# Phase 1 reads x by features for its last five pairs of token tiles: no transposes on TensorE, one multiplication on VectorE

## The chip, the cores and the metric

The kernel runs on one core of one Trainium2 chip. The metric is the device time of one execution, in microseconds (us). Lower is better.

## The reference

One transformer block over S = 2048 tokens of width D = 640, in float32. The change touches only the first line of the work: the layer norm of x, and the three projections that read it.

```python
mod = (silu(c) @ w_mod).reshape(6 parts of 640)      # sa, ca, ga, sb, cb, gb
h = layernorm(x) * (1 + ca) + sa                     # phase 1 starts here
q, k, v = h @ wqkv                                   # 32 heads of 20
phi_q, phi_k = [softmax(z), softmax(-z)] of q @ w_phi, k @ w_phi, per head
o = phi_q (phi_k^T v) / (phi_q sum(phi_k) + 1e-6)    # linear attention
x = x + ga * (o @ wo)
h = layernorm(x) * (1 + cb) + sb
x = x + gb * (relu(h @ w1 + b1)^2 @ w2 + b2)
```

layernorm subtracts the mean over the 640 features and divides by sqrt(variance + 1e-5).

## The kernel before

The 2048 tokens are 16 tiles of 128 (t = 0 to 15) and 8 pairs of tiles. Names in the code count pairs from 0: `hT7`, `xb7` belong to the pair that the title of the change calls pair 8, so its pairs 4 to 8 are j = 3 to 7. This text counts from 0 throughout.

Phase 1 makes, for every tile, k, v and (up to tile 11) q. TensorE multiplies with the tokens as the stationary operand, so it needs the normed x with features on partitions. That is `hT[j]`: five chunks of 128 features, each in a high part (rounded) and a low part (the rest), for the 256 tokens of a pair. Each product is three matmuls (high with high, high with low, low with high), and the third one of a chunk reads the low part. `proj` does one tile: 15 matmuls of 384 columns, then 15 of 256.

How `hT` comes about before the change. `load_x` brings 256 tokens (tokens on partitions). `ln_parts` gets mean and variance by accumulating activations on ScalarE (L339, L344), the small arithmetic on GpSimd, and then normalises in place on ScalarE (L350). `t1(j, chunks)` transposes a chunk on TensorE (L363, two 128x128 per chunk, into the PSUM tile `ta`), and `t_out` takes it out: ScalarE scales and shifts it (L374, to `hfa`), ScalarE rounds it to the high part (L375, to `hT`), and VectorE subtracts to get the low part (`lo`, L89 `hT<-hfa,hT`).

Around it, per tile: ScalarE copies k and q out of PSUM (L431) and v into `vt` (L424 to L427). VectorE takes each head's maximum and minimum (L435, L436: `mxk`, `mxq`), subtracts them (L438: `ek`, `eq`, two each), ScalarE takes exponentials (L441, L442), and VectorE sums k's (`sk`, L446), inverts (L447) and multiplies (L448), and sums q's (`rs_q`, L483). `do_kv` multiplies `ek` with `vt` into `kvp`, two tiles at a time, at every even tile from 2 on between its v and its q. On the side run the modulation vectors (`wm`, L295 and L297 on VectorE; `mc` and a last column on TensorE) and, from tile 9 on, the weights of the output projection (`rwo`, `wo`). Tiles 12 to 15 get their q after phase 1.

The order of the work in this stretch: TensorE's is as written in the code (`manual_schedule`). On VectorE, ScalarE, GpSimd and SyncE a scheduler sorts the instructions when the kernel is built, within the constraints of `tc.issue_after`. What comes out is one fixed queue per engine: an instruction that waits holds up all that stand behind it. The tags of the tiles set the number of buffers: `ek` has two, `hT` two, XB two.

Of the kernel before, what the change touches and what calls it, by code (L numbers as in the profile page):

```python
# [8 lines left out]
F32 = mybir.dt.float32  # L9
# [24 lines left out]
POSTPONED = 4  # L34
WARM = 9
KEPT = NT - POSTPONED
W2_AT = 48
PLAIN = 2
DEALT = range(NT // 2)
# [13 lines left out]
def kernel(  # L53
    ctx: ExitStack,
    tc: tile.TileContext,
    x: bass.AP,
    wk5: bass.AP,
    wk1: bass.AP,
    wq5: bass.AP,
# [79 lines left out]
    def tp(name):  # L139
        return psA.tile([P, 512], F32, tag="tp", name=name)  # L140
# [78 lines left out]
                nc.sync.dma_start(raw[nm][2][:40, 1], w1)  # L219

    def load_x(j):
        XB[j] = tok2(f"x{j % 2}", f"xb{j}")
        nc.sync.dma_start(XB[j], x[256 * j : 256 * j + 256].rearrange("(i p) d -> p i d", p=P))

    def load_wm(d):
        WM[d] = flat(tok2(("k", "k", "q0", "q1", "w")[d], f"wm_{d}"))
# [74 lines left out]
    def mod_turn(part, p, *cs_):  # L301
        t = MT.setdefault(part, None) or row("s1", f"mt{part}")
        MT[part] = t
        a, n = cs_[0] * P, len(cs_) * P
        for i, c in enumerate(cs_):
            src = by_turn(MA[part])[:, c] if part in (3, 4) else MA[part][:, c * P : (c + 1) * P]
            nc.tensor.transpose(p[:, i * P : (i + 1) * P], src, ident)
        nc.scalar.activation(t[:, a : a + n], p[:, :n], AF.Copy)
# [24 lines left out]
    def ln_parts(xt, nm, spare=None):  # L333
# [16 lines left out]
            nc.scalar.activation(xt[:, i], xt[:, i], AF.Identity, bias=nb[:, i : i + 1], scale=sq[:, i : i + 1])  # L350
        yield

    def layer_norm(xt, nm, spare=None):
        for _ in ln_parts(xt, nm, spare):
            pass
# [29 lines left out]

    DONE = []

    def t1(j, *ds, more=None):
        if 0 in ds:
            HT[j] = ht(f"hT{j}", j)  # L390
        p = tp(f"ta{j}_{ds[0]}")
        for k, d in enumerate(ds):
            t_in(XB[j], d, p[:, 256 * k : 256 * k + 256])
        if more:
            mod_turn(more[0], p[:, 256:], 4)
# [3 lines left out]
        if more:  # L399
            mod_sum(*more)  # L400

    def proj(nm, t, between=None):
        p = pj(f"p{nm}{t}")
# [123 lines left out]
    def wo_weights(*gs):  # L527
# [189 lines left out]
    pe.__enter__()  # L717
    for t in range(2, NT - 2):
        j, i = divmod(t, 2)
        if i == 0 and j < NT // 2 - 2:  # L720
            load_x(j + 2)
        PK[t] = row("s2", f"k{t}")
        to_sb(proj("k", t), PK[t])
        if t == NT - 4:
            t1(j + 1, 0, 1)
        norm = j + 1 if i == 0 and t < NT - 4 else j + 2 if t == NT - 5 else None
        if norm:
            if not i:
                parts = ln_parts(XB[norm], f"a{norm}")
            with tc.issue_after(newest(ET_.Activation)):  # L730
                next(parts)
        p = proj("v", t, (1, 0, lambda: t1(j + 1, 4)) if t == NT - 3 else None)
# [6 lines left out]
        if norm and not i:  # L739
# [4 lines left out]
        if norm and not i:  # L744
            next(parts)
        if i and t < NT - 4:
            t1(j + 1, 2, 3)
        with tc.issue_after(newest(ET_.DVE)):
            k_norm(EK[t], t)
        if t < NT - POSTPONED:  # L750
            do_q(t, (1, 3, lambda: t1(j + 1, 4, more=LAST_COL.get(t))) if i else None)
            if norm and i:
                with tc.issue_after(newest(ET_.Activation)), tc.issue_after(DONE[0]):
                    next(parts)
            if i:
                with tc.issue_after(DONE[1]):
                    q_chain(t)
            else:
                q_chain(t)
        if i == 0 and t < NT - 4:  # L760
            t1(j + 1, 0, 1)
        if t == NT - 6:
            parts = ln_parts(XB[j + 2], f"a{j + 2}")
            with tc.issue_after(newest(ET_.Activation)):
                next(parts)
        SIDE[t]()
    pe.__exit__(None, None, None)
    behind.close()
# [944 lines left out]
    by_hand.__exit__(None, None, None)  # L1713


_INS = ["x", "wk5", "wk1", "wq5", "wq1", "wv", "bd", "c", "w_ss", "w_mod", "wo", "w1", "b1", "w2", "b2"]


# [53 lines left out]
```

## Time and profile before

| | us |
|---|---|
| three runs | 755.70, 755.99, 756.49 |
| median of the runs | 755.99 |
| span of the profiled execution | 754.9 |
| TensorE busy in the span | 749.6 (99%) |
| VectorE busy | 607.5 (80%) |
| ScalarE busy | 458.8 (61%) |
| GpSimd busy | 170.4 (23%) |

The profile gives no time of its own for the profiled execution beside its span; the median of the runs is 1.1 us above the span, and that is taken as what lies around it. The granted TensorE clock is 1.000 throughout. Phase 1 with the five pairs in question lies at about 92 to 233 us of the span. "Busy" counts overlapped instructions once; a matmul's end is modelled, so that a TensorE that is always busy may still issue more slowly than it could. In the rows below, the columns are start, duration, engine, line, operation, output and inputs, count, and in brackets the idle time of the engine before it and who ended it.

### The profile page before, as it was taken

The page shows a single profiled execution, that of the slowest core. Times are in us where ns is not written, and L with a number is a line of the kernel's source. Part 1 is how long each engine was busy: PE and PEld are TensorE (multiplying, and loading weights), DVE is VectorE, ACT ScalarE, POOL GpSimd, SP SyncE. Part 2 cuts the span into 40 slices and gives each one's busy share as a digit, 9 for nine tenths or more (in the row PEclk, how much of TensorE's full clock was granted, in tenths as well). Part 3 has the DMA queues.
Part 4 walks back from the last instruction along what each step waited for, and adds up shares of the span by engine and source line. Part 5 has one row for each costly group of instructions (what it writes and reads, how often), then busy time and mean ns, then how long its engine had stood idle before and what let it go on. Part 6 is the DMA issues. An engine that isn't in the chain of part 4 may idle for free.

```text
span 754.9 us, 15404 instructions
## 1 busy us (share of the span) xinstructions
PE 749.6 (99%) x5888; PEld 731.9 (97%) x5888; DVE 607.5 (80%) x1123; ACT 458.8 (61%) x1060; POOL 170.4 (23%) x365
## 2 busy tenths in 40 slices
PE   9999999999999999999999999999999999999998
PEld 9999999999999998998899999999999999999997
DVE  6598987988999899999755768787777776777766
ACT  5767666677863355556677757485574756647431
POOL 3001101011200237646303030132221313213110
PEclk9999999999999999999999999999999999999999
DMA  9811431342432264664777475897677767667461
GB/s 324 336 39 80 155 96 70 106 139 103 138 105 93 71 190 142 143 153 124 173 204 218 121 216 215 278 326 204 185 213 204 205 196 212 191 181 208 132 188 36
DMA packets 58931, 126.70 MB, mean 168 GB/s; under 512 B 7452, under 2 KB 16417, under 8 KB 58857
## 3 DMA queue, kind: packets, MB, share of 16 engines
q1 hardware_dynamic: 38706, 79.41, 32.1%
q0 software_dynamic: 17568, 41.00, 22.0%
q10 hardware_dynamic: 2583, 5.30, 1.9%
q8 instruction: 46, 0.75, 0.5%
q14 instruction: 28, 0.23, 0.1%
HBM read 100.94 MB, written 29.89 MB: 173 GB/s over the span
## 4 chain that ended last, share of the span: by engine, by line
PE 86%; DVE 11%; POOL 1%; issue 1%; ACT 0%; DVEq 0%; POOLq 0%
PE up L79 24%; PE acc L79 18%; PE pk L79 9%; PE pv L79 9%; PE pq L79 8%; PE acc3x L79 5%; PE pwo L79 3%; PE kvp L455 3%; DVE dn L883 3%; DVE scr L881 2%; DVE ezb L905 2%; PE foldk L281 1%; PE ta L363 1%; DVE ot L89 1%; POOL dn L889 1%; PE foldq L281 1%
## 5 line engine op out<-in xcount | busy, mean ns | idle before, releaser
L79 PE MATMUL up<-h,w 128*128 128x256 f32 x1640 | 204.4, 276 | 0.1
L79 PEld LDWEIGHTS up<-h,w 128*128 128x128 f32 x1640 | 196.4, 188 | 0.5 <-DVE h L89 0.3
L1321 ACT ACTIVATE ft<-up,b_t 128x256 f32<-128x256 f32 x104 | 48.9, 471 | 96.0 <-PE up L79 95.6
L79 PE MATMUL acc<-w,ra 128*128 128x384 f32 x452 | 97.5, 335 | 0.0
L79 PE MATMUL pwo<-wo,ot 128*128 128x256 f32 (+3 forms) x512 | 79.9, 311 | 0.4 <-DVE ot L89 0.4
L1322 DVE TENSOR_TENSOR ft<-ft 128x256 f32<-128x256 f32 x104 | 43.8, 421 | 43.0 <-ACT ft L1321 41.4
L79 PEld LDWEIGHTS pwo<-wo,ot 128*128 128x128 f32 (+1 forms) x512 | 74.3, 188 | 3.5 <-issue 2.7
L79 PE MATMUL pq<-wq,hT 128*128 128x384 f32 (+1 forms) x480 | 75.1, 311 | 0.0
L79 PEld LDWEIGHTS acc<-w,ra 128*128 128x128 f32 x452 | 72.7, 188 | 0.9 <-DVE ra L89 0.6
L79 PE MATMUL pk<-wk,hT 128*128 128x384 f32 (+1 forms) x480 | 72.7, 308 | 0.0
L79 PE MATMUL pv<-wv,hT 128*128 128x384 f32 (+1 forms) x480 | 71.6, 306 | 0.0
L79 PEld LDWEIGHTS pq<-wq,hT 128*128 128x128 f32 x480 | 71.0, 188 | 0.6 <-issue 0.2
L79 PEld LDWEIGHTS pk<-wk,hT 128*128 128x128 f32 x480 | 70.5, 188 | 0.4 <-issue 0.2
L79 PEld LDWEIGHTS pv<-wv,hT 128*128 128x128 f32 x480 | 70.0, 188 | 0.0
L89 DVE TENSOR_TENSOR ra<-ft,ra 128x384 fp32r<-128x384 f32 (+2 forms) x86 | 36.8, 449 | 32.7 <-ACT ra L1345 19.4
L1431 POOL DMA_DIRECT2D ring_a<-td_a x34 | 18.5, 544 | 117.1 <-PE acc L79 103.7
L1345 ACT ACTIVATE ra<-ft 128x384 fp32r<-128x384 f32 x48 | 25.2, 526 | 28.5 <-DVE ft L1322 22.4
L79 PE MATMUL acc3x<-w,ra 128*128 128x256 f32 x231 | 39.5, 278 | 0.0
L79 PEld LDWEIGHTS acc3x<-w,ra 128*128 128x128 f32 x231 | 37.2, 188 | 0.0
L1336 DVE TENSOR_TENSOR ft<-ft 128x128 f32<-128x128 f32 x136 | 33.4, 286 | 1.2
L446 DVE TENSOR_REDUCE sk<-ek 128x64 f32<-128x1280 f32 x16 | 23.7, 1483 | 12.4 <-ACT ek L441 10.8
L889 POOL TENSOR_TENSOR dn<-dn,rs_q 128x32 f32<-128x32 f32 x32 | 19.9, 622 | 59.0 <-DVE dn L883 58.7
(264 smaller groups left out, 1458.2 us busy)
## 6 DMA issues: line engine op xcount, KB each, us to landing
ring_c<-td_c POOLq DMA_DIRECT2D x34, 384.0 KB, 4.1
ring_a<-td_a POOLq DMA_DIRECT2D x34, 384.0 KB, 3.5
ring_b<-td_b POOLq DMA_DIRECT2D x34, 256.0 KB, 3.5
esp<-eq SPq DMA_DIRECT2D x12, 640.0 KB, 3.2
el<-esp SPq DMA_DIRECT2D x12, 640.0 KB, 4.4
rw<-in_w SPq DMA_DIRECT2D x23, 320.0 KB, 3.5
wm<-in_w_mod SPq DMA_DIRECT2D x20, 320.0 KB, 3.7
xb<-in_x SPq DMA_DIRECT2D x8, 640.0 KB, 4.0
```

The costliest lines, as they stand in the source:

```text
L79: nc.tensor.matmul(o, a, b, start=first and i == 0, stop=last and i == len(terms) - 1, skip_group_check=skip,)
L89: (eng or nc.vector).tensor_tensor(out_lo, full, hi.bitcast(F32), op=ALU.subtract)
L281: nc.tensor.matmul(p[g // 3][:, (g % 3) * 120 : (g % 3) * 120 + n], r, bd_t[:120, g * 120 : g * 120 + n], start=True, stop=True,)
L446: nc.vector.tensor_reduce(s, heads(flat(e)), axis=AX.X, op=ALU.add)
L455: nc.tensor.matmul(kvp[g // 4][64 * c : 64 * c + 64, a : a + 2 * n].rearrange("p (s n) -> p s n", s=2), v[:, u], e[:, :, o : o + n], start ...
L883: nc.vector.tensor_reduce(dn.rearrange("p s h -> p (s h)"), heads(z), axis=AX.X, op=ALU.add)
L889: nc.gpsimd.tensor_tensor(dn[:, s], dn[:, s], rs[:, 1 - s], op=ALU.mult)
L1321: nc.scalar.activation(r, p, AF.Relu, bias=b1_t[:, f : f + 1])
L1322: nc.vector.tensor_tensor(r, r, r, op=ALU.mult)
L1336: nc.vector.tensor_tensor(t[:, o], t[:, a], t[:, b], op=op)
L1345: nc.scalar.activation(a[:, 0, :3], t[:, :3], AF.Copy)
L1431: nc.gpsimd.dma_start(RING[j, n, r], TD[n][r].bitcast(F32R))
```

## The change

For pairs 3 to 7, x is also given to the kernel as `x_t`, transposed on the host's side of the input list (features on partitions, 256 tokens in a row). What is done with it:

- `row_parts(j)`: tokens are still loaded (`load_x`, always into the buffer x1) and still go through the two accumulating passes on ScalarE, but only for the statistics. The pass that normalised them is gone. Two small DMAs (`put_rows`) write minus the mean and one over the deviation, a row of 256 numbers each, to DRAM.
- `put_mean(j)`: a DMA from DRAM to DRAM spreads minus the mean over a 128 x 1280 buffer `xd`. `centre(j)`: a DMA issued on GpSimd adds `x_t` to it.
- `load_xt(j)`: a pair later, the centred x comes in as `xt`, and the row of one over the deviation, on all partitions, as `rb`.
- `t1(j, chunks)`: one VectorE multiplication of all five chunks (128 x 1280) by `rb`, in place; then `t_out` reads `xt` where it read PSUM. Chunks 0 to 2 are emitted at the end of the even tile, 3 and 4 in the odd tile, ahead of its spread.
- The last column of the modulation vectors, which shared a transposing group with chunk 4, is a group of its own (`last_col`). The special handling of the last pair (its statistics and chunks earlier than the others', for tiles 11 to 13) is gone: it now runs in the same places as the others.

```diff
+TURNED = 3
+    def put_rows(j, *cols):
+        LR[j] = dram.tile([2, 256], F32, name=f"lr{j}")
+        for k, col in enumerate(cols):
+            nc.sync.dma_start(LR[j][k].rearrange("(i p) -> p i", p=P), col)
+    def put_mean(j):
+        XD[j] = dram.tile([P, NC * 256], F32, name=f"xd{j}")
+        nc.sync.dma_start(
+            XD[j].rearrange("p (d n) -> p d n", d=NC), LR[j][0][None, None, :].to_broadcast([P, NC, 256])
+        )
+    def centre(j):
+        nc.gpsimd.dma_start(XD[j], x_t[j * P : (j + 1) * P], accum_op=ALU.add, max_dma_last_dim=2048)
+    def load_xt(j):
+        XT[j] = flat(tok2("x0", f"xt{j}")).rearrange("p (d n) -> p d n", d=NC)
+        nc.sync.dma_start(XT[j], XD[j].rearrange("p (d n) -> p d n", d=NC))
+        RB[j] = row("s3", f"rb{j}")[:, :256]
+        nc.sync.dma_start(RB[j], LR[j][1][None, :].to_broadcast([P, 256]))
...
+    def row_parts(j):
...
+        for i in range(2):
+            nc.scalar.activation(xt[:, i], xt[:, i], AF.Identity, accum_out=sm[:, i : i + 1])
...
+        for i in range(2):
+            nc.scalar.activation(xt[:, i], xt[:, i], AF.Square, bias=sm[:, i : i + 1], accum_out=sq[:, i : i + 1])
...
+        put_rows(j, sm, sq)
...
-    def t1(j, *ds, more=None):
+    def t1(j, *ds):
...
+        if j >= TURNED:
+            if 0 in ds:
+                with tc.issue_after(newest(ET_.DVE)):
+                    nc.vector.tensor_tensor(XT[j], XT[j], RB[j][:, None, :].to_broadcast([P, NC, 256]), op=ALU.mult)
+            with tc.issue_after(newest(ET_.Activation)):
+                for d in ds:
+                    t_out(cols_a, HT[j], d, f"a{j}", XT[j][:, d], XT[j][:, d])
+            return
         p = tp(f"ta{j}_{ds[0]}")
         for k, d in enumerate(ds):
             t_in(XB[j], d, p[:, 256 * k : 256 * k + 256])
...
-        12: lambda: t1(NT // 2 - 1, 2, 3),
...
     for t in range(2, NT - 2):
         j, i = divmod(t, 2)
-        if i == 0 and j < NT // 2 - 2:
-            load_x(j + 2)
+        norm_by_tokens = j + 1 < TURNED
+        norm = i == 0 and norm_by_tokens
+        new_x = TURNED if norm else j + 3 if i and TURNED < j + 3 < NT // 2 else None
+        centred = TURNED if j + 2 == TURNED and i else j + 2 if TURNED < j + 2 < NT // 2 and not i else None
+        if new_x:
+            load_x(new_x)
+        if centred:
+            put_mean(centred)
+        if i == 0 and j + 1 >= TURNED:
+            load_xt(j + 1)
...
-        if t == NT - 4:
-            t1(j + 1, 0, 1)
-        norm = j + 1 if i == 0 and t < NT - 4 else j + 2 if t == NT - 5 else None
...
+        if i and not norm_by_tokens:
+            t1(j + 1, 3, 4)
         spread(PK[t], EK[t], f"k{t}")
         exps(EK[t])
...
+        if centred:
+            centre(centred)
...
+        if new_x:
+            with tc.issue_after(newest(ET_.Activation)):
+                row_parts(new_x)
+        if i == 0:
+            t1(j + 1, 0, 1, *(() if norm_by_tokens else (2,)))
```

Three places show how the queues change. In the rows, the number behind a name is the tile's or the pair's, and what follows the underscore tells buffers apart; `xt6` and `hT6` are the x and the features of pair 6, which TensorE reads from tile 12 on.

The first place is VectorE's queue in tile 11, where pair 6 is made ready. Before:

```order
L89 TENSOR_TENSOR hT6_2381<-hfa6_0_2387,hT6_2381 128x256
L89 TENSOR_TENSOR hT6_2381<-hfa6_1_2391,hT6_2381 128x256
L504 TENSOR_TENSOR rwo2_2401<-rwo2_2401,ga_b_220 128x640
L438 TENSOR_TENSOR eq10_2371<-q10_2368,mxq10_2372 128x640
L435 TENSOR_REDUCE mxk11_2488<-k11_2409 128x32
L436 TENSOR_REDUCE mxk11_2488<-k11_2409 128x32
L438 TENSOR_TENSOR ek11_2487<-k11_2409,mxk11_2488 128x640
L89 TENSOR_TENSOR wo2_2405<-rwo2_2401,wo2_2405 128x640
L438 TENSOR_TENSOR ek11_2487<-k11_2409,mxk11_2488 128x640
L483 TENSOR_REDUCE rs_q_106<-eq10_2371 128x64
L89 TENSOR_TENSOR hT6_2381<-hfa6_2_2500,hT6_2381 128x256
L89 TENSOR_TENSOR hT6_2381<-hfa6_3_2504,hT6_2381 128x256
```

and now:

```order
L435 TENSOR_TENSOR xt6_2201<-xt6_2201,rb6_2203 128x1280
L484 TENSOR_TENSOR ek11_2453<-k11_2382,mxk11_2460 128x640 x2
L91 TENSOR_TENSOR hT6_2363<-xt6_2201,hT6_2363 128x256 x2
L481 TENSOR_REDUCE mxq11_2511<-q11_2507 128x32
L482 TENSOR_REDUCE mxq11_2511<-q11_2507 128x32
L492 TENSOR_REDUCE sk11_2467<-ek11_2453 128x64
L91 TENSOR_TENSOR hT6_2363<-xt6_2201,hT6_2363 128x256
L550 TENSOR_TENSOR rwo2_2374<-rwo2_2374,ga_b_220 128x640
L484 TENSOR_TENSOR eq11_2510<-q11_2507,mxq11_2511 128x640
L91 TENSOR_TENSOR hT6_2363<-xt6_2201,hT6_2363 128x256 x2
```

All five low parts of pair 6 now stand behind the subtractions of `ek11`, three of them behind the sum `sk11` as well; before, two stood ahead of `mxk11` and four ahead of `sk11`.

The second place is VectorE's queue in tiles 12 and 13, where the last pair is made ready. Before, two more low parts of `hT7` stand just ahead of the first row:

```order
L483 TENSOR_REDUCE rs_q_106<-eq11_2559 128x64
L438 TENSOR_TENSOR ek12_2689<-k12_2569,mxk12_2690 128x640 x2
L89 TENSOR_TENSOR wo4_2714<-rwo4_2710,wo4_2714 128x640
L89 TENSOR_TENSOR hT7_2604<-hfa7_2_2677,hT7_2604 128x256
L89 TENSOR_TENSOR hT7_2604<-hfa7_3_2681,hT7_2604 128x256
L446 TENSOR_REDUCE sk12_2697<-ek12_2689 128x64
L447 RECIPROCAL sk12_2697<-sk12_2697 128x64
L435 TENSOR_REDUCE mxk13_2797<-k13_2718 128x32
L436 TENSOR_REDUCE mxk13_2797<-k13_2718 128x32
L448 TENSOR_TENSOR ek12_2689<-ek12_2689,sk12_2697 128x1280
L438 TENSOR_TENSOR ek13_2796<-k13_2718,mxk13_2797 128x640 x2
L89 TENSOR_TENSOR hT7_2604<-hfa7_4_2773,hT7_2604 128x256
```

and now:

```order
L493 RECIPROCAL sk12_2625<-sk12_2625 128x64
L494 TENSOR_TENSOR ek12_2617<-ek12_2617,sk12_2625 128x1280
L435 TENSOR_TENSOR xt7_2520<-xt7_2520,rb7_2522 128x1280
L481 TENSOR_REDUCE mxk13_2735<-k13_2657 128x32
L482 TENSOR_REDUCE mxk13_2735<-k13_2657 128x32
L484 TENSOR_TENSOR ek13_2728<-k13_2657,mxk13_2735 128x640 x2
L91 TENSOR_TENSOR hT7_2629<-xt7_2520,hT7_2629 128x256 x3
L492 TENSOR_REDUCE sk13_2742<-ek13_2728 128x64
L91 TENSOR_TENSOR hT7_2629<-xt7_2520,hT7_2629 128x256 x2
```

The five low parts of the last pair all follow `ek13` now, two of them `sk13`; before, four were done before `sk12` and only one followed `ek13`.

The third place is ScalarE's queue in tile 11. Before:

```order
L441 ACTIVATE ek11_2487<-ek11_2487 128x640
L374 ACTIVATE hfa6_2_2500<-ta6_2_2495,cols_a_100 128x256
L374 ACTIVATE hfa6_3_2504<-ta6_2_2495,cols_a_100 128x256
L442 ACTIVATE ek11_2487<-ek11_2487 128x640
L375 ACTIVATE hT6_2381<-hfa6_2_2500 128x256
L375 ACTIVATE hT6_2381<-hfa6_3_2504 128x256
```

and now:

```order
L477 ACTIVATE q11_2507<-pq11_0_2471 128x384
L411 ACTIVATE xt6_2201<-xt6_2201,cols_a_100 128x256 x5
L332 ACTIVATE mt4_2295<-ml4_2491 128x128
L412 ACTIVATE hT6_2363<-xt6_2201 128x256
L487 ACTIVATE ek11_2453<-ek11_2453 128x640
L412 ACTIVATE hT6_2363<-xt6_2201 128x256
L477 ACTIVATE q11_2507<-pq11_1_2472 128x256
L488 ACTIVATE ek11_2453<-ek11_2453 128x640
L412 ACTIVATE hT6_2363<-xt6_2201 128x256 x3
```

The scalings of all five chunks now run in one batch before the first rounding, and the exponentials of `ek11` stand between the roundings.

More of the change, by code (lines that the diff above doesn't have):

```diff
@@ L386, with last_col @@
     DONE = []
-    def t1(j, *ds, more=None):
+    def last_col(part, dest):
+        mod_turn(part, tp(f"ml{part}"), 4)
+        mod_sum(part, dest)
+    def t1(j, *ds):
         if 0 in ds:
             HT[j] = ht(f"hT{j}", j)
+        if j >= TURNED:
[5 more added lines that the diff above has]
+                    t_out(cols_a, HT[j], d, f"a{j}", XT[j][:, d], XT[j][:, d])
+            DONE[:] = newest(ET_.Activation), newest(ET_.DVE)
+            return
         p = tp(f"ta{j}_{ds[0]}")
@@ L738 @@
         v_out(t, p)
-        if norm and not i:
+        if norm:
             next(parts)
         EK[t] = tok2("k", f"ek{t}")
+        if i and not norm_by_tokens:
+            t1(j + 1, 3, 4)
         spread(PK[t], EK[t], f"k{t}")
         exps(EK[t])
-        if norm and not i:
+        if norm:
             next(parts)
-        if i and t < NT - 4:
+        if centred:
+            centre(centred)
+        if i and norm_by_tokens:
             t1(j + 1, 2, 3)
@@ L750 @@
         if t < NT - POSTPONED:
[L751 to L755, printed above, removed]
+            if i and norm_by_tokens:
+                do_q(t, (1, 3, lambda: t1(j + 1, 4)))
                 with tc.issue_after(DONE[1]):
```

28 lines of the change are left out of this document (14 added, 14 removed).

## The prediction

> **What bounds the kernel now.** I read the page first, then busy time by stage, the waits, and the timelines of VectorE and TensorE at the end of phase 1. The page says TensorE:
>
> ```profile
> PE 749.6 (99%) x5888; PEld 731.9 (97%) x5888; DVE 607.5 (80%) x1123; ACT 458.8 (61%) x1060; POOL 170.4 (23%) x365
> ```
>
> The busy times of the stage of the five pairs, up to where the last pair's features are due (columns: length, then PE, PEld, DVE, ACT, POOL busy), and what VectorE waited for there:
>
> ```profile
> 90.90:222.00 131.10, 131.10 (x1049) 130.14 (x1049) 117.60 (x153) 90.22 (x205) 15.28 (x24) 1.00 0.34 110
> ...
> DVE sk L446 <- ACT ek L441: 8.5, 5, 2.9
> DVE rs_q L483 <- ACT eq L442: 2.0, 3, 1.0
> DVE hT L89 <- ACT hT L375: 1.9, 4, 0.8
> ```
>
> TensorE never pauses, but VectorE is busy 117.6 of 131.1 us. Its whole idle time is 13.5 us, of which these three waits, all for ScalarE, make 12.4. So two engines are close to the bound, and the 80% of the page hides it. How close shows at the last pair (VectorE, then TensorE):
>
> ```profile
> 212.58 0.75 DVE L89 TENSOR_TENSOR hT<-hfa,hT 128x256 fp32r<-128x256 f32 x2
> 213.25 1.48 DVE L483 TENSOR_REDUCE rs_q<-eq 128x64 f32<-128x1280 f32 x1
> ...
> 220.25 0.76 DVE L435 TENSOR_REDUCE mxk<-k 128x32 f32<-128x640 f32 x1
> 220.93 0.80 DVE L436 TENSOR_REDUCE mxk<-k 128x32 f32<-128x640 f32 x1
> 221.65 1.48 DVE L448 TENSOR_TENSOR ek<-ek,sk 128x1280 f32<-128x1280 f32 x1
> 223.05 1.55 DVE L438 TENSOR_TENSOR ek<-k,mxk 128x640 f32<-128x640 f32 x2
> 224.52 0.42 DVE L89 TENSOR_TENSOR hT<-hfa,hT 128x256 fp32r<-128x256 f32 x1
> 226.04 1.49 DVE L446 TENSOR_REDUCE sk<-ek 128x64 f32<-128x1280 f32 x1 [1.10 <-ACT ek L442]
> ...
> 219.52 2.76 PE L79 MATMUL pv<-wv,hT 128*128 128x384 f32 x15
> 224.10 8.76 PE L79 MATMUL pk<-wk,hT 128*128 128x384 f32 x60
> 232.80 2.54 PE L455 MATMUL kvp<-ek,vt 128*64 128x120 f32 x44
> ```
>
> TensorE begins tile 14's k, the first user of `hT7`, at 224.10, and VectorE writes the last low part at 224.52 to 224.94, only just in time: 15 matmuls of 384 columns take about 2.6 us (the v row is 2.76, its end modelled), and the last chunk is their last fifth.
>
> **What goes on TensorE.** The chain of waits from 92 to 232.8 us, 140.8 us, by line:
>
> ```profile
> by line: PE pk L79 33.9%; PE pv L79 27.7%; PE pq L79 24.9%; PE kvp L455 8.0%; PE ta L363 4.0%; PE mc L307 1.4%; PE ta L307 0.2%
> ```
>
> The 50 transposes (L363) are 4.0%, 5.6 us. The modulation's last column (L307) stays. This is all that TensorE can gain: 5.6 us.
>
> **What comes on VectorE, and what stands around it.** The multiplication is a 128x1280 tensor-tensor operation with a broadcast operand, as L448 is. That one takes 1.48 us and frees the engine after 1.40 (221.65 to 223.05). Five of them are 7.0 us; subtractions for the low parts stay as many. So VectorE has 7.0 us more work where TensorE wants everything 5.6 us earlier: 12.6 us to find in 13.5 us of idle time. Which idle time goes? In tile 6:
>
> ```profile
> 123.14 1.55 DVE L438 TENSOR_TENSOR ek<-k,mxk 128x640 f32<-128x640 f32 x2
> 124.04 1.74 ACT L350 ACTIVATE xb<-xb,nba,sqa 128x640 f32<-128x640 f32 x2 [1.57 <-POOL nba L347]
> 126.16 0.73 ACT L442 ACTIVATE ek<-ek 128x640 f32<-128x640 f32 x1
> 127.55 1.49 DVE L446 TENSOR_REDUCE sk<-ek 128x64 f32<-128x1280 f32 x1 [2.86 <-ACT ek L441]
> ```
>
> At every even tile ScalarE normalises x (L350, 1.74 us) between VectorE's subtraction and the exponential it waits for. That pass is gone, so the long waits for `ek` (8.5 us over five tiles) mostly go. In their place come waits for ScalarE's batch:
>
> ```profile
> 128.63 1.02 ACT L374 ACTIVATE hfa<-ta,cols_a 128x256 f32<-128x256 f32 x2
> 129.54 0.72 ACT L375 ACTIVATE hT<-hfa 128x256 fp32r<-128x256 f32 x2
> ```
>
> A scaling costs 0.46 us (129.54 less 128.63, halved), a rounding 0.31. These are from PSUM and SBUF; a scaling from SBUF is not in the trace at this size, its bounds are the rounding's 0.31 and 0.46, and I take the upper, being the same operation. The new queues run five scalings, 2.3 us, and a rounding before the first low part, against VectorE's own 1.5 us (`ek`) or 2.9 us (`mxk` and `ek`) after the multiplication. Laid out on the new queues with these steps, VectorE's new waits are:
>
> - tile 7: 1.15 for the first rounding, then 0.6 and 0.3, since exponentials stand between roundings: 2.05
> - tile 9: 0.7 and 0.3: 1.0
> - tile 11: ScalarE takes out the first half of q11 first, which TensorE has not finished, and the last column: 2.25, then 0.6: 2.85
> - even tiles: `sk8` has nothing between it and `ek8`, and ScalarE still has statistics and a modulation row in front: 1.3; the first output weight in tile 10: 0.6; `ek4` for `kvp`: 0.4
> - waits for TensorE's k7 and for q4's exponential behind k5's copy, 1.1 each: 2.2
>
> Together N = 10.4 us, against 13.5 before.
>
> **The sum, at the last pair.** Before, L448 for tile 12 ends at 223.05. Ahead of it stand two operations on `mxk13` (1.40) and four low parts (1.34) that now come later: 220.3 in the new order. Add four earlier multiplications, 5.6: 225.9; less the idle time that goes, 13.5 - N. Then come the fifth multiplication 1.40, `mxk13` 1.40 and `ek13` 1.47 (223.05 to 224.52), three low parts 1.0 (0.335 each, two in 212.58 to 213.25), `sk13` with a wait of 1.35 for its exponentials (ScalarE: five scalings, three roundings, v's copies, two exponentials, 5.3 us after the multiplication) and 1.40, and the fourth low part 0.34: 234.3 - (13.5 - N) = 220.8 + N. From there TensorE has four matmuls of 384 columns, 0.7 us, to the end of the first half; before that was at 224.27 + 2.6 = 226.9 (the chain below puts the start of `pk14` at 224.27). So the change is 221.5 + N - 226.9 = N - 5.4, and with N = 10.4 it is +5.0 us. Behind this point nothing gives it back, by the chain of waits:
>
> ```profile
> 224.27 8.60 PE pk L79 x60
> 232.87 2.47 PE kvp L455 x43
> ...
> 250.98 1.79 PE pq L79 x9
> 252.76 1.05 PE z L823 x4
> 253.82 0.36 ACT zb L833
> ```
>
> TensorE runs through to `z` with its order and length unchanged, and VectorE's and ScalarE's first work of phase 2 follows from `z`; whatever `pk14` is late, they are late. Against the span of 754.9 that is 759.9, and with the 1.1 us between span and median, 761.0.
>
> Ends: with N = 0, no idle time at all, -5.4, which meets TensorE's own limit of -5.6; with N as before, 13.5, +8.1.
>
> **The rest, at nothing, and why.** ScalarE loses L350 and keeps the statistics, which it does earlier: 90.2 us busy in 131.1 leaves room. GpSimd loses a small multiplication per pair and gains one DMA; it is busy 15.3 us in the stage. SyncE issues five more DMAs per pair. The nearest rows for their times:
>
> ```profile
> xb<-in_x SPq DMA_DIRECT2D x8, 640.0 KB, 4.0
> a<-in_x POOLq DMA_DIRECT2D x16, 320.0 KB, 6.6
> ga_b<-gate SPq DMA_DIRECT2D x1, 320.0 KB, 3.9
> ```
>
> A pair's chain is: rows, at most 4.0; mean spread, twice the 320 KB row, 7.8; accumulation, at most twice 6.6, 13.2; load, 4.0: 29 us as an upper estimate. Pair 6's statistics end with tile 7 and its multiplication opens tile 11; three tiles, about 45 us, lie between. For pair 3 it is two tiles, 30 us, so that by this estimate it is only just in time. In SyncE's queue `load_xt` waits for the buffer x0 of the pair before and holds up `esp` stores and weight loads behind it, whose users come a tile or more later. DMA share is 0.34 there. If that cover were gone, the multiplication would hold VectorE's whole queue.
>
> **Rivals.**
>
> A, the forecast: VectorE's queue with ScalarE's batch sets the pace: 761.0.
>
> B, faster: VectorE's idle time closes further than I lay out, because it becomes the bound and ScalarE then runs ahead of it. Decided at N = 5.4; with N = 2.5 (only tile 7's and part of the others' waits left) it gives -2.9: 753.1. At its limit TensorE alone decides, 755.99 - 5.6 = 750.4. For it: no wait of TensorE in the whole stage before. Against: the 12.6 us needed are nearly all that there is. The Trainium skill's Perfetto Trace Analysis, section Identifying the Most-Contended Engine, says to optimise first the engine with the highest occupancy; by that rule TensorE's 5.6 us would be had in full. The trace agrees on TensorE's occupancy; the 90% of VectorE in the stage is what the rule leaves out.
>
> C, no change: N near 5.4, gain and new waits cancel: 756.0.
>
> D, later still: an x comes late, because a wait in SyncE's queue holds up `load_xt`. Each microsecond beyond the cover is one lost; 4 us more gives 765.0. For it: four DMAs in a row, each behind the last, and pair 3's short cover. Against: for the later pairs some 15 us to spare.
>
> The Trainium skill's TensorE: Matmul & The Clock Gate, section Why this matters for your kernels, warns of pauses of TensorE above about 3 us, after which its throughput drops. By that rule the new pauses could cost more than their own length; how much, no row here can say, since TensorE never pauses in this stage and the granted clock is 1.00 in the row of the stage.
>
> **Numbers.** A measurement of this kernel tells 0.2%, 1.5 us, from no change. A 0.62, B 0.18, C 0.14, D 0.06. Faster is B; same is C; slower is A and D, 0.68. The range reaches from 754.0 (N = 3.4, most of B left out) to 765.0 (D's beginning, N = 14.4); A's own is 757.6 to 764, for N from 7 to 13.4.
>
> **What would show it.** The `ta` group of L363 has 10 instructions instead of 60. TensorE waits for VectorE's `hT` at the start of tiles 8, 12 and 14, in pieces of 0.5 to 3 us, together 10.6 us: the 5.6 that it saves and 5.0 more. VectorE is busy 91% or more of the stage, and its waits move from `sk` to `hT`. `ek` at even tiles waits under 1 us. The start of the second `kvp` from the end, 232.80, moves to about 238. I am wrong if TensorE shows no wait for `hT` (B), if VectorE's idle time in the stage is below 5 us, or if the multiplication itself is seen waiting for a DMA (D).

## The result: 78 us slower, and the profile after

The changed kernel takes 834.03 us (median of four runs, 829.09 to 836.05) against 756.24 for the kernel before on the same chip: ratio 1.102, 95% interval 1.0985 to 1.1055. The profiled execution is the one of 829.09 us, the fastest of the four; its span is 827.4, 72.5 above the span before. The forecast was 761.0, its range 754 to 765.

The engines on the page after, and two of its stretches of 30 us (columns as in the prediction's stage row: length, PE, PEld, DVE, ACT, POOL busy, granted clock, DMA share, GB/s):

```profile
PE 765.4 (93%) x5838; PEld 740.3 (89%) x5838; DVE 615.0 (74%) x1128; ACT 449.1 (54%) x1050; POOL 171.2 (21%) x365
...
120.00:150.00 30.00, 8.96 (x35) 7.45 (x36) 10.34 (x16) 5.45 (x14) 1.04 (x1) 0.60 0.70 116
150.00:180.00 30.00, 26.76 (x206) 25.58 (x205) 22.06 (x28) 16.58 (x41) 2.16 (x4) 1.00 0.74 119
```

TensorE never paused in this stage before. Now it idles, and in the first of the two stretches no engine is busy for more than 10.34 of 30 us. Nearly all of the loss lies in phase 1. The `kvp` that began at 232.80 begins here:

```profile
304.46 2.54 PE L501 MATMUL kvp<-ek,vt 128*64 128x120 f32 x44
```

That is 71.7 us later: 33.1 of them are lost by tile 6 (its `kvp` begins at 153.74 instead of 120.64), 31.6 from tile 6 to tile 12, and 7.0 behind it. From the last `kvp` on the rest takes about as long as before (507.2 us, then 506.5). VectorE's longest waits between 60 and 330 us, and its wait for x (engine, line, what it waited for: us, times, longest):

```profile
DVE wm L321 <- DMA wm<-in_w_mod: 29.1, 4, 19.3
DVE rwo L550 <- DMA rwo<-in_wo: 19.8, 4, 7.8
...
DVE xt L435 <- DMA xt<-xd: 1.7, 1, 1.7
```

This is the surprise. The multiplication hardly ever waits for its x. VectorE waits for loads that the change doesn't touch, the modulation's weights (`wm`) and the output's (`rwo`). The longest of these waits, from the timelines of SyncE (its DMA issues), VectorE and TensorE:

```profile
111.07 0.33 SPq L245 DMA_DIRECT2D xt<-xd  x1
...
111.94 0.43 SPq L232 DMA_DIRECT2D lr<-sma  x1
112.47 1.48 SPq L225 DMA_DIRECT2D xb<-in_x  x1
122.77 0.55 SPq L236 DMA_DIRECT2D xd<-lr  x1
123.37 0.63 SPq L232 DMA_DIRECT2D lr<-sqa  x1
124.09 2.54 SPq L340 DMA_DIRECT2D wm<-in_w_mod  x2
140.17 0.33 SPq L247 DMA_DIRECT2D rb<-lr  x1
...
142.10 0.89 DVE L321 SCALAR_TENSOR_TENSOR wm<-wm,cs,wm 128x640 f32<-128x640 f32 x1 [19.34 <-DMA wm<-in_w_mod]
...
144.30 0.41 DVE L91 TENSOR_TENSOR hT<-xt,hT 128x256 fp32r<-128x256 f32 x1
...
144.77 3.89 PE L81 MATMUL pk<-wk,hT 128*128 128x384 f32 x16 [20.71 <-DVE hT L91]
```

SyncE writes the mean's row at 111.94 and stops until it has landed (122.77), issues the spread, the second row and the `wm` loads, and stops until the second row has landed (140.17). The `wm` load issued at 124.09 is there at 142.10. The last low part of `hT` stands behind the sum that needs it, and TensorE waits 20.7 us for that low part. Over the stage (60 to 310 us) SyncE stands 103 us in such waits for rows to land:

```profile
SPq L247 <- DMA lr<-sqa: 57.5, 5, 13.5
SPq L236 <- DMA lr<-sma: 45.9, 5, 11.0
```

How such a transfer holds the queue shows at the first pair, where little else is under way (a row write is issued at 75.83, the spread at 84.65, the load of x by tokens at 85.39):

```profile
76.00:84.00 8.00, 8.00 (x59) 8.00 (x58) 7.14 (x10) 6.33 (x17) 3.04 (x2) 1.00 0.07 22
84.00:96.00 12.00, 12.00 (x109) 11.78 (x109) 10.16 (x13) 2.14 (x4) 0.00 (x0) 1.00 0.23 59
96.00:100.00 4.00, 1.88 (x16) 1.69 (x15) 0.00 (x0) 0.39 (x1) 1.20 (x1) 1.00 0.82 310
```

While the row of 256 elements of 4 bytes is out, 8.8 us, the DMA engines are 7% busy (0.00 from 77.50 to 84.50 us). Then the spread moves at 59 GB/s for some 11 us, and what stands behind it flows only after it, at 310 GB/s. The `wm` and `xb` loads behind take about three times as long from issue to landing as before, here of after (last column, us):

```profile
wm<-in_w_mod SPq DMA_DIRECT2D x15, 320.0 KB, 8.6
xd<-lr SPq DMA_DIRECT2D x5, 640.0 KB, 12.3
...
xb<-in_x SPq DMA_DIRECT2D x4, 640.0 KB, 14.0
```

The prediction's row for the same `xb` load before has 4.0; `wm` took 3.0.

### The profile page after: what moved, and what is told of

Same layout as the page of the kernel before. It is cut to its first block, busy times and chain, and to the rows that moved or that the text cites. A ratio compares the mean times of both kernels' runs of the same rounds, so it can differ in the third digit from the quotient of the medians.

```text
span 827.4 us, 15346 instructions
## 1 busy us (share of the span) xinstructions
PE 765.4 (93%) x5838; PEld 740.3 (89%) x5838; DVE 615.0 (74%) x1128; ACT 449.1 (54%) x1050; POOL 171.2 (21%) x365
## 4 chain that ended last, share of the span: by engine, by line
PE 65%; DMA 13%; DVE 10%; issue 7%; ACT 4%; SPq 1%; POOL 0%; DVEq 0%; POOLq 0%; ACTq 0%
PE up L81 22%; PE acc L81 16%; PE pwo L81 5%; PE acc3x L81 4%; PE pq L81 4%; DMA lr<-sqa 4%; PE pk L81 4%; DMA xb<-in_x 3%; PE pv L81 3%; DMA wm<-in_w_mod 2%; DMA rwo<-in_wo 2%; PE te L975 1%; DVE ezb L955 1%; DVE dn L933 1%; DVE scr L931 1%
## 5 line engine op out<-in xcount | busy, mean ns | idle before, releaser
L81 PE MATMUL pk<-wk,hT 128*128 128x384 f32 (+1 forms) x480 | 88.4, 344 | 48.5 <-DVE hT L91 30.6
L81 PEld LDWEIGHTS pk<-wk,hT 128*128 128x128 f32 x480 | 79.9, 214 | 55.9 <-DVE hT L91 34.4
L81 PE MATMUL pv<-wv,hT 128*128 128x384 f32 (+1 forms) x480 | 74.8, 315 | 6.1 <-ACT q L477 6.1
L81 PEld LDWEIGHTS pv<-wv,hT 128*128 128x128 f32 x480 | 73.3, 196 | 6.4 <-ACT q L477 6.4
L1372 DVE TENSOR_TENSOR ft<-ft 128x256 f32<-128x256 f32 x104 | 43.8, 421 | 43.6 <-ACT ft L1371 42.1
L91 DVE TENSOR_TENSOR ra<-ft,ra 128x384 fp32r<-128x384 f32 (+2 forms) x86 | 36.8, 449 | 32.7 <-ACT ra L1395 19.4
L477 ACT ACTIVATE k<-pk 128x384 f32<-128x384 f32 (+1 forms) x32 | 13.4, 434 | 54.6 <-PE pk L81 54.6
L321 DVE SCALAR_TENSOR_TENSOR wm<-wm,cs,wm 128x640 f32<-128x640 f32 x16 | 14.1, 879 | 29.1 <-DMA wm<-in_w_mod 29.1
```

The costliest lines, as they stand in the source:

```text
L81: nc.tensor.matmul(o, a, b, start=first and i == 0, stop=last and i == len(terms) - 1, skip_group_check=skip,)
L91: (eng or nc.vector).tensor_tensor(out_lo, full, hi.bitcast(F32), op=ALU.subtract)
L321: nc.vector.scalar_tensor_tensor(acc, t, cs[:, k : k + 1], prev, op0=ALU.mult, op1=ALU.add)
L477: nc.scalar.activation(t[:, a:b], p[h][:, : b - a], AF.Copy)
L1372: nc.vector.tensor_tensor(r, r, r, op=ALU.mult)
```

## The experiments

All times are medians; "kvp" is the start of the second `kvp` from the end. Each ratio is to runs of the kernel before in the same series (756.1 to 756.5).

| run | us | ratio, 95% interval | kvp |
|---|---|---|---|
| before / after | 756.24 / 834.03 | 1.102 (1.0985 to 1.1055) | 232.80 / 304.46 |
| e1 no chain | 764.83 | 1.0116 (1.0099 to 1.0134) | 239.61 |
| e2 rows only | 769.95 | 1.0195 (1.0167 to 1.0224) | 244.04 |
| e3 centring only, waiting for nothing | 791.29 | 1.0461 (1.0439 to 1.0483) | 266.34 |
| e5 before, with rows | 771.01 | 1.0194 (1.0178 to 1.0209) | 247.97 |
| e6 rows on GpSimd | 791.5 | 1.0454 (1.0434 to 1.0475) | 267.58 |
| e8 spread on GpSimd | 827.91 | 1.0953 (1.0913 to 1.0993) | 301.70 |
| e7 chain on GpSimd | 820.0 | 1.0843 (1.0809 to 1.0878) | 294.83 |
| e10 no chain, GpSimd multiplies | 757.51 | 1.0011 (0.9997 to 1.0026) | 232.24 |
| e16 as e10, last pair VectorE | 759.47 | 1.0044 (1.0026 to 1.0061) | 233.15 |
| e11 late loads unread | 816.17 | 1.0783 (1.0752 to 1.0814) | 291.30 |
| e12 late loads on ScalarE | 840.52 | 1.1109 (1.1070 to 1.1148) | 310.86 |
| e13 rows ahead of x | 836.53 | 1.1055 (1.1033 to 1.1077) | 312.47 |
| e15 x not waiting | 834.16 | 1.1024 (1.1000 to 1.1048) | 309.11 |
| e20 and no accumulation | 818.64 | 1.0824 (1.0800 to 1.0848) | 296.43 |
| e19 and a fifth of the spread | 790.19 | 1.0425 (1.0390 to 1.0460) | 264.03 |
| e17 one row of two | 804.41 | 1.0638 (1.0616 to 1.0660) | 277.21 |
| e4 rows in 512-byte pieces | 789.26 | 1.0432 (1.0404 to 1.0461) | 257.69 |
| e18 e4 without centring | 784.19 | 1.0373 (1.0356 to 1.0390) | 251.46 |

**e1, the forecast's own term by itself.** All compute engines keep the changed kernel's order.

```diff
-        nc.sync.dma_start(XT[j], XD[j]...)        # rows, spread and accumulation gone too
+        nc.sync.dma_start(XT[j], x_t[j * P : (j + 1) * P]...)
-        nc.sync.dma_start(RB[j], LR[j][1]...)
+        nc.sync.dma_start(RB[j], x_t[j * P, :256]...)
```

> The changed kernel with its compute engines' order untouched, but x by features and the row of scales are loaded from inputs, so neither waits for the statistics: no row writes, no spread of the mean, no accumulation (x is left uncentred and is multiplied by a row of x instead of 1/deviation). Theory 1, late x: all of the loss beyond the forecast's own term is waiting for x's chain of DMAs; then what is left is the forecast's term, VectorE's queue: 761 us (757.6 to 764), TensorE waiting for hT at tiles 8, 12 and 14. Rival, TensorE only saves its transposes: 750 to 753. Rival, VectorE's queue itself was mis-sized: above 770.

764.83: 8.7 us above before, 69 below after. So, by difference, the chain of DMAs costs 69 of the 78 us, and the new order on VectorE 8.7 where the forecast had 5.0; that is just above its own range of 757.6 to 764. TensorE waits 7.3 us for `hT` here (forecast 10.6). VectorE's waits for ScalarE's batch in this run, by its timeline:

```profile
138.94 0.43 DVE L91 TENSOR_TENSOR hT<-xt,hT 128x256 fp32r<-128x256 f32 x1 [1.48 <-ACT hT L411]
139.88 0.43 DVE L91 TENSOR_TENSOR hT<-xt,hT 128x256 fp32r<-128x256 f32 x1 [0.51 <-ACT hT L411]
...
169.98 1.10 DVE L91 TENSOR_TENSOR hT<-xt,hT 128x256 fp32r<-128x256 f32 x3 [0.96 <-ACT hT L411]
...
201.98 0.43 DVE L91 TENSOR_TENSOR hT<-xt,hT 128x256 fp32r<-128x256 f32 x1 [2.84 <-ACT hT L411]
202.91 0.42 DVE L91 TENSOR_TENSOR hT<-xt,hT 128x256 fp32r<-128x256 f32 x1 [0.51 <-ACT hT L411]
```

**e2 and e3, the chain's halves.** e2 keeps `put_rows` and drops `put_mean` and `centre`; e3 drops `put_rows` and spreads a row of an input.

> The changed kernel with the statistics written to DRAM as rows and the row of scales read back as before, but x by features is loaded straight from its input, without spread and accumulation (x is left uncentred). Theory 1a, the row writes of 4-byte elements hold SyncE's queue: most of the 78 us stay, 800 us or more. Theory 1b, the spread and the accumulation are what comes late: within 8 us of the run without any chain, so 755 to 770.

> The changed kernel without the row writes: the mean's spread is taken from a row of an input and the row of scales likewise, so spread, accumulation and load of x are kept but wait for no statistics (what is added to x is not its mean). Theory 1a, row writes: within 10 us of the run without any chain, 755 to 775. Theory 1b, spread and accumulation: most of the 78 us stay, 800 us or more.

1a falls: alone, the rows cost 5.1 us more than no chain. That is what 1b expected of e2, but e3, which was to show its other half, tells nothing of the stage. Its spreads and accumulations wait for no statistics, so they ran early, and its whole 26.5 us are one stall before tile 4's `kvp` (117.20 against 90.53 in e1, and the same distance from there on). GpSimd stood before the issue of an accumulation, with pair 2's statistics behind it in its queue:

```profile
ACT junka L368 <- POOL sma L364: 20.8, 1, 20.8
```

**e5, the rows added to the kernel before.**

```diff
+        if nm in ("a3", "a4", "a5", "a6", "a7"):
+            lr = dram.tile([2, 256], F32, name=f"lr{nm}")
+            for k, col in enumerate((sm, sq)):
+                nc.sync.dma_start(lr[k].rearrange("(i p) -> p i", p=P), col)
```

> The kernel before, with the two row writes of the statistics of pairs 3 to 7 added on SyncE's queue and read by nobody. Theory 1a, each row write holds the queue for 7 to 18 us and what stands behind it comes late: 10 to 40 us slower, 766 to 796, with VectorE waiting for modulation and output weights. Theory 1b, or a queue whose followers have room: within 2 us of 756.

15 us, as 1a expected, with VectorE waiting 17.1 us for `wm` and a `wm` load taking 12.8 us instead of 3.0. Ten writes of 1 KB that nobody reads delay what stands behind them.

**e6, e8, e7, the chain's DMAs on another queue** (`nc.sync` to `nc.gpsimd` in `put_rows`; in `put_mean`; in all of `put_rows`, `put_mean`, `load_xt`).

> The changed kernel with the two row writes of each pair issued on GpSimd's queue; spread, load of x and row of scales stay on SyncE's queue, which still waits there for rows and accumulation. Theory 2, SyncE's queue delays the loads behind the chain (the modulation's weights, whose users stand ahead of hT in VectorE's queue): two parts of it, the small elements on the queue's DMAs and SyncE's waits, and here only the first goes: 790 to 820. Theory 3, x itself is late because its chain is longer than its cover: no change, 825 to 840.

> The changed kernel with the mean's spread issued on GpSimd's queue, which waits for the row there; rows, x and the row of scales stay on SyncE's queue. Theory 2: one of the three waits of each pair leaves SyncE's queue and the 640 KB spread no longer stands ahead of the modulation's loads: 780 to 810. Theory 3: 825 to 840, the chain being as long.

> The changed kernel with all DMAs of x's chain (rows, spread, accumulation, load of x, row of scales) on GpSimd's queue: SyncE's queue carries what it carried before the change, less five passes nothing. Theory 2: the loads of weights are on time again and what is left is the run without any chain, 765, and a few us for x: 764 to 775. Theory 3, x's chain is too long for its cover: 800 us or more, with the multiplication waiting for a DMA.

Rows off SyncE's queue give 42 us back, as theory 2 said. The spread gives 6, less than it said, and the whole chain 14, where theory 2 had 764 to 775. Both times lie in theory 3's ranges, but not by its mechanism: the multiplication waits 0.8 us for its x in e8 and not at all in e7. In e8 SyncE stands 45.7 us at its row writes, for statistics that GpSimd makes behind the spread in its own queue. In e7 the waits had moved into GpSimd's queue, where the statistics' small operations stand behind the chain, and ScalarE waits for them:

```profile
ACT xb L385 <- POOL sma L383: 49.3, 4, 22.6
```

**e11 and e12, the late loads.** e11 sends them to DRAM tiles that nobody reads; e12 issues them on ScalarE's queue (`nc.scalar.dma_start` in `stage`, `prep_wo` and `load_x`).

> The changed kernel, but the loads of the modulation's and the output's weights during phase 1 go to DRAM tiles that nobody reads, and VectorE's sums and products take a constant in their place (the modulation and the output weights are left out so). SyncE's queue has the same loads in the same places, x's chain is as it was. Theory 2, what comes late are those loads, 29 us of waits for the modulation's and 20 for the output's weights in VectorE's queue: 775 to 795. Theory 3, x's chain of four DMAs is itself too long: 815 or more, and the multiplication waits for x instead.

> The changed kernel with the loads of modulation weights, output weights and x by tokens issued on ScalarE's queue, so that x's chain has SyncE's queue nearly for itself. Theory 2: these loads are on time and most of the loss goes: 765 to 790. Theory 3: 815 or more. A rival against both: ScalarE stops at a load whose buffer is not free and pays with its own queue: above 800, with ScalarE idle at the loads.

In e11 VectorE no longer waits for weights, yet only 18 us come back. 816.17 is in theory 3's range, but the multiplication does not wait for x either (0.2 us); now ScalarE waits for x by tokens, whose load stands behind the same chain:

```profile
ACT xb L393 <- DMA xb<-in_x: 35.1, 4, 11.5
```

So the weights were only the first to be late. e12 is the rival named there: ScalarE stands still for 20.7 us ahead of a copy of k, with loads before it in its queue and no other wait that the profile names, and TensorE waits 14.7 us for that copy.

**e13 and e15, order and waiting.** Here I had a new theory: chains of 34 to 38 us one after another, too long for a pair's 30.

```diff
+            with tc.issue_after(newest(ET_.SP)):        # e13: x behind the next pair's row and spread
                 load_xt(j + 1)
-        nc.sync.dma_start(XT[j], XD[j]...)              # e15: all DMAs kept, x does not wait for the accumulation
+        nc.sync.dma_start(XT[j], x_t[j * P : (j + 1) * P]...)
```

> The changed kernel with one thing moved in SyncE's queue: the load of a pair's x (which waits for the accumulation) and its row of scales stand behind the next pair's first row write and spread instead of ahead of them. Same DMAs, same queue, same compute order. Theory 4, one chain in a row: in the changed kernel the next pair's row write is issued 0.8 to 16 us after the load of x, so chains of 34 to 38 us from row to load follow each other where TensorE needs a pair every 30 us, and everything on SyncE's queue is late with them; here two chains overlap and much goes: 770 to 800. Theory 2b, the DMAs' volume and small elements on SyncE's rings: within 10 us of 834.

> The changed kernel with all its DMAs kept (rows, spread, accumulation, load of x, row of scales), but x by features is loaded from its input, so that it does not wait for the accumulation, whose result nobody reads (x is left uncentred). Theory 5, the chain's length: row, spread, accumulation and load follow each other for 34 to 38 us on one queue, where TensorE takes a pair in 30; cut at its end, the chain on SyncE's queue is a row and a spread, some 25 us, and most of the loss goes: 765 to 785. Theory 6, the volume: row writes and spread fill SyncE's DMA rings whoever waits: 815 or more.

Neither changes the time (836.53, 834.16). In e13 the wait only moves, to the multiplication:

```profile
DVE xt L435 <- DMA rb<-lr: 61.3, 4, 22.5
```

e15 is the stronger of the two: the same DMAs, x free to come early, and the same 834. Theories 4 and 5 fall. What is left is how long the transfers hold the queue (theory 6), and SyncE's stops until the rows have landed, which e15 keeps (59.1 and 50.0 us).

**e17, e4, e18, e20, e19, the transfers made shorter.** e17 drops the second row write; e4 makes the rows on TensorE; e18 is e4 without centring; e20 is e15 without `centre`; e19 is e20 with a fifth of the spread.

```diff
-        put_rows(j, sm, sq)                              # e17
+        put_rows(j, sm)
+            nc.tensor.transpose(p[:2, :P], col, ident)   # e4: two rows of 512 bytes each
+            nc.scalar.activation(r, p[:2, :P], AF.Copy)
+            nc.sync.dma_start(LR[j][k].rearrange("(i p) -> i p", p=P), r)
-            XD[j]..., LR[j][0]....to_broadcast([P, NC, 256])   # e19, against e20
+            XD[j][:, :256], LR[j][0]....to_broadcast([P, 256])
```

> The changed kernel with one row write of each pair instead of two: the row of the mean stays, that of 1/deviation goes and the row of scales is read from an input (x is scaled by a wrong row). Theory 6, transfers one behind another: by the traces a pair's transfers take 11 us without the chain (DMA share 0.37 of 30 us), a row write 8.8 alone, the spread 11; after the change 11 + 17.6 + 11 = 40 us a pair, against 30 that TensorE needs and 41 that it took from tile 6 to 12. With one row 31, about even: 770 to 795. Rival, each row write delays what stands behind it by its own length, full or not: half of what the 512-byte rows gave, 805 to 820.

> The changed kernel with the rows of statistics made by two small transposes on TensorE and a copy on ScalarE, and written as two runs of 512 bytes instead of 256 elements of 4 bytes; they are made in the tile behind, where the spread is issued; all else, with spread, accumulation and SyncE's waits, as in the changed kernel. Theory 2a, the rows of 4-byte elements are what fills SyncE's queue: 764 to 778. Theory 2b, SyncE's waits in order and the spread do it: 790 to 830.

> The run with rows made by TensorE's transposes and written in 512-byte pieces, without spread and accumulation, x loaded from its input (x is left uncentred). It tells how much of the 33 us that were left there belongs to the centring and how much to the two small transposes, which TensorE waited for. Theory 6 has both below 30 us a pair (11 + 11 with the centring), so the transposes cost most of it: 775 to 790. Rival, the centring in DRAM costs by itself: 765 to 772.

> The run in which x does not wait for the accumulation, and now without the accumulation: both row writes and the whole spread stay (x is left uncentred). Theory 6, SyncE's queue serves its transfers one behind another, and the accumulation is not among them: nothing changes, 820 to 838. Rival, the accumulation's 13 us of traffic a pair slows the others: 775 to 810.

> As the run without accumulation, but the spread writes one of five chunks, 128 KB instead of 640 KB, in the same place of the queue, so its transfer shrinks from 11 us to an estimated 2.2. Theory 6: 9 us a pair taken from the spread count like the 9 us of a row write, whose removal gave 30: 790 to 812. Rival, the row writes alone hold the queue and the spread's size matters little: 820 or more.

One row less: 29.6 us back. Four fifths of the spread less (e20 to e19): 28.5 back, at the lower edge of theory 6's range. One takes a write of 1 KB from SyncE's queue (8.8 us at the first pair), the other 512 KB (the spread's landing falls from 13.1 to 5.4 us after its issue), and over the kernel they count alike. That is theory 6's main claim. Only e19 shows it by itself: e17 also takes away SyncE's stop for that row (57.5 us in the changed kernel), while in e19 SyncE's stops for both rows hardly change (101.5 us, 110.4 in e20). e2 speaks against the stops as the whole cause: SyncE stops 61.1 us for its second rows, and it costs 5.1. A run with rows and spread kept and no stop for them was not made.

Theory 6's sum was too smooth: e17 should have come to 795 at most and was 804, and e4 to 764 to 778 by 2a and was 789. e18 explains e4 in part. Without centring 784 remain, 19.4 above e1. By the traces 6.0 of these are lost by tile 4, where TensorE waits ahead of its new transposes, 5.7 more by the last `kvp`, and some 8 behind phase 1, where nothing was edited; why is open. The wait before tile 4:

```profile
PE st L233 <- POOL sqa L391: 3.3, 1, 3.3
```

With 512-byte rows the centring costs only 5.1 us. So the 4-byte rows without centring (e2 over e1) and the centring with short rows (e4 over e18) cost about 5 us each, and the two together 69: neither is dear until the queue has both.

e20's 818.64 lies just under its range: the accumulation costs 15.5 us though it is on GpSimd's queue. Whether its traffic does it, or GpSimd's standing before it until the spread has landed (121.6 us in e15), was not separated.

**e10 and e16, what the change would give if the chain cost nothing.**

```diff
-                with tc.issue_after(newest(ET_.DVE)):
-                    nc.vector.tensor_tensor(XT[j], XT[j], RB[j]..., op=ALU.mult)
+                nc.gpsimd.tensor_tensor(XT[j], XT[j], RB[j]..., op=ALU.mult)
```

> The run without any chain (x uncentred, scaled by a row of an input) with the five multiplications on GpSimd instead of VectorE. Forecast's theory, VectorE's queue is what the new order waits for, 7.0 us of it the multiplications: 765 falls by about 7 to 11 us, to 754 to 758. Rival, ScalarE's batch of scalings and roundings sets the pace, not VectorE: 762 to 766. Rival, GpSimd is slow at 128x1280 and becomes the new wait: above 770, with TensorE waiting for hT behind GpSimd.

> The run without any chain (x uncentred, scaled by a row of an input), with the multiplications of four pairs on GpSimd and that of the last pair on VectorE. In the run with all five on GpSimd, TensorE was 5.7 us ahead of the kernel before at tile 12 and lost 5.2 at the last pair, where VectorE's two subtractions for q11 took 4.3 us beside GpSimd's multiplication instead of 1.5. If that is what it lost, 753 to 755; rival, VectorE's queue at the last pair is late whoever multiplies: 757 to 759. A limit for the change with a chain that costs nothing.

757.51: not distinguishable from before. e16 went the rival's way, slightly above its 759. No run here is faster than the kernel before.

## Why the prediction was wrong, point by point

**The step that failed: "The rest, at nothing".** The DMAs on SyncE's queue were put at nothing and cost 69 us (after less e1). Two things in it.

First, a row write was bounded by "at most 4.0", the time of a 640 KB load. The nearest row was another one, in the trace of before: the modulation's gate is written from 128 partitions to a row in DRAM, 640 elements of 4 bytes, and its reader is the next DMA that SyncE issues (SyncE's timeline of before):

```profile
144.26 0.38 SPq L330 DMA_DIRECT2D gate<-gate_a  x1
154.62 0.34 SPq L331 DMA_DIRECT2D ga_b<-gate  x1
```

From issue to issue that is 10.4 us (8.3 in the changed kernel, where the profile names the wait for the landing). The first rows of the five pairs took 7.5 to 12.1, the second ones, behind the spread, 15.8 (median). The prediction's 4.0 also stood for both rows together. The Trainium skill's DMA: Bandwidth & Descriptors, section Specifications, says that transfers below 512 B are off line rate, with a read-modify-write. The traces agree that the small pieces are slow: 8.8 us for 256 elements of 4 bytes with the queue to itself, 4.0 in e4 for two rows in 512-byte pieces (issued at 79.02, their reader at 82.98); a read-modify-write no run here shows.

The spread was taken as twice a 320 KB load, 7.8; it took 12.3. The accumulation's upper end, 13.2, was about right (9.5 to 14.3 from its issue to the load of x). From the first row to the load of x the chain took 33.8 to 38.4 us, where the estimate has 25; even so the multiplication waited for x only once, 1.7 us.

Second, and this is worth more, the chain was weighed only against the lead that x has. "Holds up `esp` stores and weight loads behind it, whose users come a tile or more later" was written down and not priced. By e1's DMA shares (0.32 to 0.42 of 30 us) a pair's transfers take 11 us. Two rows of 8.8 and a spread of 11 make that 40, and TensorE needs a pair every 30. From tile 6 to tile 12 the changed kernel took 41.0 us a pair (`kvp` at 153.74 and 276.87, three pairs). The same page's section Queues, rings and completion order says that on each DMA engine the descriptors of a queue's ring are consumed in ring order; the x by tokens issued at 85.39 and flowing from 96 on agrees. A queue that is over its time is late with everything, and the first victim here was `wm`.

The same sum for the other runs (an estimate: 11 without a chain, 8.8 for a 4-byte row, 4 for both 512-byte rows, 11 for the spread, 2.2 for a fifth of it), beside the measured time of a pair from tile 6 to tile 12:

| run | sum, us | measured, us |
|---|---|---|
| e1 | 11 | 32.3 |
| e18 | 15 | 31.9 |
| e4 | 26 | 33.8 |
| e2 | 29 | 33.1 |
| e19 | 31 | 36.3 |
| e17 | 31 | 36.9 |
| after, e15, e20 | 40 | 41.0, 42.0, 42.1 |

With a sum below 30 the chain costs at most 1.9 us a pair (e4 over e18), above it 4 to 10. e5, in the order of before, does not fit: 28 by its sum (0.34 of 30 us, and two rows), 35.4 measured.

**Rival D** had the place, SyncE's queue, and not the victim or the size. It named a late x, and the multiplication waits 1.7 us. It priced 4 us beyond the cover; lost were 33.1 us by tile 6, 20.7 of them in one stall, and then 10.5 a pair up to tile 12.

**The forecast's own term held in its mechanism, as e1 shows, and was sized too small (8.7 for 5.0).** The waits laid out were 2.05 in tile 7, 1.0 in tile 9, 2.85 in tile 11; measured 1.99, 0.96 and 3.35. N was 10.4; VectorE's idle time in e1 to the last pair is 11.7:

```profile
90.60:228.80 138.20, 132.90 (x1020) 128.21 (x1020) 126.54 (x160) 79.28 (x192) 11.98 (x16) 0.98 0.38 123
```

It is busy 126.54 of 138.20, 92%, as forecast. The second `kvp` from the end moved by 6.8 (forecast 5.2); with N at 11.7 the prediction's formula, N - 5.4, gives 6.3. The forecast has no term for TensorE's clock, which falls in tile 12:

```profile
204.00:208.00 4.00, 2.33 (x5) 1.32 (x5) 4.00 (x7) 1.41 (x4) 0.00 (x0) 0.50 0.00 0
208.00:212.00 4.00, 3.62 (x20) 3.62 (x21) 4.00 (x7) 1.88 (x4) 0.00 (x0) 0.69 0.56 186
```

At half and at 0.69 of full speed, 2.33 and 3.62 us of matmuls lose 1.2 and 1.1 us by estimate. VectorE is busy throughout these 8 us, so that the slow clock made the kernel late is not shown. Nor does TensorE's account close: 5.6 saved and 6.8 later make 12.4 us, of which waits for `hT` are 7.3 and the clock 2.3. The rule on pauses that the prediction cited from the Trainium skill (TensorE: Matmul & The Clock Gate, above about 3 us) holds after the changed kernel's pause of 20.7 us, where the clock is 0.50 as well. In e1 no pause there is longer than 1.69 us, so here the measurement is stricter than the rule. Pauses of 0.23, 1.16 and 0.94 us at e1's last pair left the clock at 1.00.

**Rival B** fell: it needed N below 5.4, and e1 has 11.7. Even with the chain free and VectorE relieved (e10), TensorE gained its 5.7 us up to tile 12 and lost 5.2 at the last pair, 3.5 of them waiting for VectorE's `hT`. e16 loses as much there with that multiplication back on VectorE.

**What stays open.** e19 shows that the length of a transfer on SyncE's queue counts, and e2 and e4 that neither half of the chain costs much alone. The sum is no formula: where it has 31, e17 and e19 took 36.9 and 36.3 us a pair. How e17's 29.6 us divide between the row's transfer and SyncE's stop for it is open. Why the same transfers on GpSimd's queue cost nearly as much (e7, e8) was not separated: GpSimd's own waits took over there.

## What to carry to other kernels

A DMA that is added to a queue has two prices: the lead of its own user, and the time for which it holds everything behind it. Add up what each queue carries in one period of the loop and compare that with the period before asking whether the new data comes in time. When a trace has no row of the new transfer's kind, look for one of its shape (elements of 4 bytes, partitions to a row), not of its size.

## What the runs showed of the hardware

- A DMA of 1 KB, 256 elements of 4 bytes, took 8.8 us with the queue to itself, about what 512 KB of a spread add to its landing (13.1 against 5.4 us). Ten of them, read by nobody, made the kernel before 15 us slower (e5), with `wm` loads behind them landing 12.8 us after issue instead of 3.0.
- A spread that reads one row of 1 KB 640 times moves 59 GB/s; the loads behind it 310 (first pair of the changed kernel).
- GpSimd's multiplication of 128x1280 can nearly stop VectorE (e10):

```profile
203.87 4.29 DVE L482 TENSOR_TENSOR eq<-q,mxq 128x640 f32<-128x640 f32 x2
...
204.03 3.44 POOL L433 TENSOR_TENSOR xt<-xt,rb 128x1280 f32<-128x1280 f32 x1 [17.58 <-DVE cols_b L336]
```

Two subtractions that take 1.55 us elsewhere took 4.29, and 4.30 at the first pair. At the other three pairs the multiplication ran mostly beside reductions, which kept their 0.81 us. The Trainium skill's SBUF — State Buffer, section Who interferes with whom, says that a VectorE instruction with two SBUF inputs contends with a GpSimd instruction that reads SBUF; the row agrees.
